# One more tile of attention's result turned by DMA, and three small moves, in a one-core transformer block

## The chip, the cores and the metric

The kernel runs on one core of a Trainium2 chip. The metric is the device time of one execution in microseconds (us); the number that counts is the median of several runs. The profile is of one further execution.

## What is computed

A pre-LayerNorm block over 2048 positions of width 512, all in float32: attention with 32 heads of 16, in which each position looks at 8 positions with a step of 2 (itself and 7 earlier ones), a projection `wo` and a residual; then an MLP of width 1792 with a squared ReLU, and a second residual.

```python
x = A_x
h = x + attention(layernorm(x), A_wqkv) @ A_wo
r = relu(layernorm(h) @ B_w1 + B_b1)
out = h + (r * r) @ B_w2 + B_b2
```

## The kernel before, in words

**Products.** Every float32 matrix is split into a high part (what the engine's float32r type keeps) and a low part (the rest), and a product is three matmul passes: high by high, low by high, high by low (`mm3`, line 231). So every operand needs a cast on ScalarE (`hi`, line 152) and a subtraction on VectorE or GpSimd (`lo`, line 155). The last group of four tiles computes its first MLP product by a Strassen-like scheme in seven products per pair of blocks (`PAIRS`, `products_a`, `products_b`, line 833); for it sums of blocks of `w1` are loaded as `traw`, summed (`t_sums`) and split (`t_split`) into `th` and `tl`, in two halves of the contraction, k = 0 and k = 2.

**Tiles.** The 2048 positions are 16 tiles of 128. First come all of the products of x with `wqkv` (to DRAM, from which attention reads its windows), then groups of four tiles go through the MLP. The attention of tiles 0 to 3 runs under the qkv products of later tiles, and tiles 0 to 3 also go through `wo` there.

**Order.** It is written out by hand. Time is cut into slots; `at`, `midway` and `after` put a chore into a slot (run before, inside or after the attention steps of that slot, by `end_slot`). VectorE's attention steps come from a generator; `pump` takes the next step while a ledger `now["dve"]` is behind `now["pe"]`. Each chore and product adds its cost in us to one of the two; `transposes` adds 0.44 to `now["pe"]` for four transposes. What an engine is given, it executes in that order.

**Turning tiles.** Attention's result `o` and the normalized `h` must be transposed before they can be stationary operands. `o_T` and `h_T` do it on TensorE into PSUM (four transposes of 128x128, line 204); ScalarE then casts the high part, VectorE subtracts for the low part. The other way is by DMA: `turn_split` copies the float32 tile into two planes of 16-bit halves (ScalarE, line 629), `turn_dma` issues a DMA transpose on the SP queue that writes back into the source (line 633), `turn_join` puts the halves together again (ScalarE, line 638), and then cast and subtraction follow from SBUF. The list `OV` names the tiles 4 to 15 that go by DMA for `o`, `HV` those for `h`. Tiles 0 to 3 of `o` go by `o_T` in slots k = 4, 5, 10, 12 (`OT`) of the last two rounds of `first_phase`; their `wo` products stand in slots k = 7, 9, 13, 15 (`WO`). Tile 3's normalized h is turned on TensorE (`h_T`) in slot 23, just before the MLP begins.

**Buffers.** Rows of 128x512 float32 come from one pool of 15 (`row`). Attention's result tiles (two tiles of 128 each), `ohl`, and blocks of `w1` share the tag "o" with three buffers.

**The deviation.** `norm_stats` computes mean and variance on VectorE; its inner `finish` computes the reciprocal deviation on GpSimd in three small instructions (lines 169 to 172) and is placed in the slot's list, for keys 6 and 10 immediately. ScalarE's `norm_apply` (line 199) waits for it.

Of the kernel before, what the change touches and what calls it, by code (L numbers as in the profile page):

```python
# [8 lines left out]
F32 = mybir.dt.float32  # L9
# [6 lines left out]
S, D, H, DH, W, F = 2048, 512, 32, 16, 8, 1792  # L16
P = 128
# [23 lines left out]
WO = 7, 9, 13, 15  # L41
HT = 20, 20, 21, 23
HK = (12, 18), (14, 19)
W2 = (18,)
LH = 3, 4, 10, 11
OP = 6, 7, 12, 13
# [12 lines left out]
def block_kernel(ctx, tc, x, wqkv, wo, w1, b1, w2, b2, out):  # L59
    nc = tc.nc  # L60
# [3 lines left out]
    att = ctx.enter_context(tc.tile_pool(name="att", bufs=2))  # L64
# [37 lines left out]
    def row(name, shape=(P, D), dt=F32):  # L102
        return work.tile(list(shape), dt, name=name, tag="row", bufs=ROWS)
# [9 lines left out]
    def at(delta, fn, *a):  # L113
        due.setdefault(now["slot"] + delta, []).append((fn, a))

    def after(delta, fn, *a):
        late.setdefault(now["slot"] + delta, []).append((fn, a))
# [4 lines left out]
    def end_slot(pe):  # L122
        now["pe"] += pe
        run(due)
        pump()
        run(amid)
        run(late)
        now["slot"] += 1
# [7 lines left out]
    def dve(t):  # L136
        now["dve"] += t
# [13 lines left out]
    def hi(dst, src):  # L151
        nc.scalar.copy(dst, src)  # L152

    def lo(eng, dst, src, h):
        eng.tensor_tensor(out=dst, in0=src, in1=h, op=ALU.subtract)  # L155
# [3 lines left out]
    def norm_stats(key, src, soon=False):  # L159
        st = small.tile([P, 6], F32, name="st")  # L160
        mv = small.tile([P, 2], F32, name="mv", bufs=4)
        rs = small.tile([P, 2], F32, name="rs", bufs=4)
        nc.vector.bn_stats(st, src)
        nc.vector.bn_aggr(mv, st)
        dve(0.93)
        stats[key] = mv, rs

        def finish():
            nc.gpsimd.tensor_scalar(out=rs[:, 1:2], in0=mv[:, 1:2], scalar1=EPS, scalar2=None,
                                    op0=ALU.add)  # L170
            nc.gpsimd.tensor_tensor(out=rs[:, 0:1], in0=rs[:, 1:2], in1=mhalf, op=ALU.pow)
            nc.gpsimd.tensor_scalar(out=rs[:, 1:2], in0=mv[:, 0:1], scalar1=rs[:, 0:1],
                                    scalar2=-1.0, op0=ALU.mult, op1=ALU.mult)
        if key in (6, 10) and soon:
            finish()
        else:
            (at if soon else after)(0, finish)
# [19 lines left out]
    def norm_apply(key, dst, src, eng):  # L197
        mv, rs = stats.pop(key)
        nc.scalar.activation(dst, src, AF.Identity, scale=rs[:, 0:1], bias=rs[:, 1:2])

    def transposes(src, banks="tr"):
        tr = turn[banks].tile("tr").rearrange("p (k c) -> p k c", k=KB)
        for k in range(KB):
            nc.tensor.transpose(tr[:, k, :], src[:, k * P:(k + 1) * P], ident)  # L204
        now["pe"] += 0.44
        return tr
# [213 lines left out]
    def pump(until=None):  # L420

        while (done[until] < G) if until is not None else (now["dve"] < now["pe"]):
            if until is None and now["dve"] > now["pe"] - HALF:
                run(amid)
            todo = sums[:]
            sums.clear()
            t = next(stream, "end")
            for a in todo:
                add_up(*a)
            if t == "end":  # L430
                now["dve"] = 1e9
                return
            if t is None:
                now["dve"] = max(now["dve"], now["pe"])
                return
            dve(t * SLOW[min(now['sub'] + 1, 2)])
# [10 lines left out]
    def x_stats(t):  # L447
        if t < XS:
            norm_stats(t, xt[t])
        else:  # L450
            act_stats(t, xt[t])
# [25 lines left out]
    def x_T(t):  # L477
        tr = transposes(xt.pop(t))
        xT[t] = row("xh", (P, KB, P), F32R), row("xl", (P, KB, P), F32R)
        at(0, hi_T, tr, [xT[t][0]])  # L480
        (midway if t >= 6 else after)(0, lo_T, tr, [xT[t][0]], [xT[t][1]])
# [112 lines left out]
    hs, hn = {}, {}  # L594
# [10 lines left out]
    def o_T(t):  # L605
        s, j = divmod(t, RI)
        pump(until=s)
        tr = transposes(o_t[s][:, j, :])
        if t % R == RI:

            ohl = att.tile([P, 2, KB, P], F32R, name="ohl", tag="o", bufs=3)
            oT[t] = ohl[:, 0], ohl[:, 1]
        else:
            oT[t] = row("oh", (P, KB, P), F32R), row("ol", (P, KB, P), F32R)
        at(0, hi_T, tr, [oT[t][0]])
        at(0, lo_T, tr, [oT[t][0]], [oT[t][1]])

    planes = {}

    def halves_of(a):  # L620
        return a.bitcast(U16).rearrange("p (n two) -> p two n", two=2)

    def two_planes(a):
        return a.bitcast(U16).rearrange("p (two n) -> p two n", two=2)

    def turn_split(key, src):

        planes[key] = src, row("pl")
        nc.scalar.copy(two_planes(planes[key][1]), halves_of(src))

    def turn_dma(key):
        src, pl = planes[key]
        nc.sync.dma_start_transpose(
            src.bitcast(U16).rearrange("p (n c) -> p n c", c=P), pl.bitcast(U16))
# [7 lines left out]
    def o_split(t):  # L642
        s, j = divmod(t, RI)
        pump(until=s)
        turn_split(("o", t), o_t[s][:, j, :])
# [12 lines left out]
    def h_split(t):  # L658
        turn_split(("h", t), hn.pop(t))
# [19 lines left out]
            norm_stats(t, h, R <= t < 14)  # L679

    def h_norm(t):
        hn[t] = row("hn")
        norm_apply(t, hn[t], hs[t], nc.scalar)
        if t >= 14 or t in (6, 10):
            h_split(t)
            turn_dma(("h", t))
# [12 lines left out]
    def wo_product(t, slots):  # L699
        ps = turn["mm"].tile("wo")  # L700
        oh, ol = oT.pop(t)
        mm3(ps, lambda k: oh[:, k, :], lambda k: ol[:, k, :],
            lambda k: wo_h[:, k, :], lambda k: wo_l[:, k, :], lows_last=t in OV)
        for n, (fn, a) in zip(slots, ((h_add, (t, ps)), (h_norm, (t,)), (add_b2, (t,)),
                                      (spill, (t,)))):
            (at if fn is h_add or fn is h_norm and t >= 14
             else midway if fn is h_norm and t in (6, 10) else after)(n + (fn is add_b2), fn, *a)
# [79 lines left out]
    def t_tile(n, name, dt=F32):  # L787
        return att.tile([P, KB, 2, P], dt, name=name, tag=("pr", "o")[n % 2], bufs=3)
# [17 lines left out]
    def t_split(n):  # L806
        h, l = t_tile(n, "th", F32R), t_tile(n, "tl", F32R)
        hi(h, tw[n])
        for k, eng in ((2, nc.gpsimd), (0, nc.vector if n < 3 else nc.gpsimd)):
            lo(eng, l[:, k:k + 2], tw[n][:, k:k + 2], h[:, k:k + 2])  # L810
        tw[n] = h, l

# [193 lines left out]
    for n in range(16):  # L1006
        gp, t = divmod(n, 4)
# [28 lines left out]
    def first_phase(t0):  # L1036
        def chores(m):
            if t0 + 3 < 16:
                if m in (0, 2):
                    at(0, x_stats, t0 + 2 + m // 2)  # L1040

                early = t0 == 12
                if m + early in ((4, 6) if t0 == R else (6, 7)):
                    at(0, x_norm, t0 + 2 + (m + early) // 7 if t0 > R else t0 + m // 2)
                if m in XT[early]:
                    x_T(t0 + 2 + XT[early].index(m))
            if t0 + 5 < 16 and m in (6, 9):
                at(0, load_x, t0 + 2 + m // 3)
            if jobs and m % 3 == 0:
                at(0, weight_job)  # L1050
            k = t0 // 2 * 12 - 72 + m
            if k == 19:
                dve(HOLD)
            for t in range(R):
                if k == OT[t]:
                    at(0, load_h, t)
                    o_T(t)
                if t in HV and k == HK[t][0]:
                    at(0, h_split, t)
                    after(0, turn_dma, ("h", t))  # L1060
                if t in HV and k == HK[t][1]:
                    at(0, turn_join, ("h", t))
                if k == WO[t]:
                    wo_product(t, (1, 3, 4, 6))
                    now["pe"] += 2.73
                if k == HT[t]:
                    (at(0, h_parts, t) if t in HV else h_T(t))
            if k in W2:
                at(0, load_w2, W2.index(k))

        def half(m):
            end_slot(1.37)
            chores(m)

        for n in range(6):
            chores(2 * n)
            qkv_of(t0 + n % 2, n // 2, lambda: half(2 * n + 1))
            end_slot(1.37)
# [40 lines left out]
    for u in range(R - 1):  # L1119
# [11 lines left out]
        for i in js:  # L1131
            t = R * (u + 1) + i
            if not end:
# [23 lines left out]
                p, h = (HP[i], i % 2) if u < 2 else HL[i]  # L1157
# [98 lines left out]
    h = hs[S // P - 1]  # L1256
# [34 lines left out]
```

## Time and profile before

| what | value |
|---|---|
| median of 3 runs | 501.62 us (501.02 to 502.49) |
| the profiled execution, its own time | 501.04 us |
| its span, first to last instruction | 499.2 us |
| TensorE, matmul / weight load | 494.5 us (99%) / 421.4 us (84%) |
| VectorE / ScalarE / GpSimd | 383.5 (77%) / 306.5 (61%) / 355.2 us (71%) |
| granted TensorE clock | 1.000 |

Around the span lie 1.84 us in which no instruction of the program runs. The engine shares are averages over the whole span; the views used further down show single stretches. In a timeline a row is a start, a duration, an engine, a line, an operation, what it writes and reads, and in brackets how long the engine stood idle before it and what ended that.

### The profile page before, as it was taken

To read this page: it belongs to the slowest core of one execution; us is meant where nothing else is said; L and a number is where in the kernel's file an instruction comes from. 1 tells how busy PE (TensorE), PEld (TensorE's weight loads), DVE (VectorE), ACT (ScalarE), POOL (GpSimd) and SP (SyncE) were. 2 spreads that over 40 slices of the span, in tenths; PEclk is the share of its full clock that TensorE was granted. 3 is DMA by queue.
4 is the path that set the end of the run, shared out by engine and by line. 5 is a ranking of instruction groups with operands and counts; after the bars stand their busy time and mean duration, and the time that the engine had idled before them with its cause. 6 is when DMAs were issued, how large, how long until landed. Compare 5 with 4: busy or idle time off the path is not lost.

```text
span 499.2 us, 7516 instructions
## 1 busy us (share of the span) xinstructions
PE 494.5 (99%) x2411; PEld 421.4 (84%) x2411; DVE 383.5 (77%) x526; ACT 306.5 (61%) x543; POOL 355.2 (71%) x429
## 2 busy tenths in 40 slices
PE   8999999999999999999999999999999999999997
PEld 8998888888888888888888888888888888998986
DVE  6379899999989899998979989897984257733233
ACT  5635777768346757478564556866454958766541
POOL 5714898896775999888878777787889353885610
PEclk9999999999999999999999999999999999999999
DMA  8668979879697889589676945977670574355212
GB/s 277 198 225 239 304 233 313 271 253 301 205 235 247 301 280 251 190 233 267 193 253 214 222 137 171 269 232 254 210 197 11 131 200 154 118 157 168 64 42 87
DMA packets 113584, 103.67 MB, mean 208 GB/s; under 512 B 33672, under 2 KB 82056, under 8 KB 113544
## 3 DMA queue, kind: packets, MB, share of 16 engines
q1 hardware_dynamic: 112600, 102.66, 68.4%
q10 hardware_dynamic: 944, 0.52, 0.3%
q8 instruction: 19, 0.31, 0.2%
q14 instruction: 21, 0.17, 0.1%
HBM read 72.65 MB, written 24.25 MB: 194 GB/s over the span
## 4 chain that ended last, share of the span: by engine, by line
PE 98%; POOL 0%; ACT 0%; issue 0%; DVE 0%; POOLq 0%; ACTq 0%
PE mm L231 49%; PE acc L920 30%; PE wo L231 9%; PE mm L833 6%; PE tr L204 2%; PE tr L974 1%; POOL tl L155 0%; PE half L943 0%; ACT th L152 0%; DVE h L945 0%; POOL ident masks.py:199 0%; POOL ident masks.py:197 0%; POOLq masks.py:199 0%; ACTq L152 0%; POOLq L957 0%
## 5 line engine op out<-in xcount | busy, mean ns | idle before, releaser
L414 POOL TENSOR_TENSOR pr<-pr 128x512 f32<-128x512 f32 (+1 forms) x128 | 134.2, 1048 | 35.9 <-DVE pr L357 30.6
L231 PE MATMUL mm<-big_l,w_h 128*128 128x512 f32 x336 | 88.5, 389 | 0.0
L357 DVE TENSOR_TENSOR pr<-ex,v 128x1024 f32<-128x1024 f32 x62 | 75.6, 1221 | 10.7 <-POOL o L414 8.1
L344 DVE TENSOR_TENSOR pr<-qp,k 128x1024 f32<-128x1024 f32 x64 | 76.8, 1201 | 5.7 <-ACT qp L271 3.5
L380 DVE TENSOR_REDUCE ex<-pr 128x64 f32<-128x1024 f32 x64 | 78.4, 1225 | 1.8
L231 PEld LDWEIGHTS mm<-big_l,w_h 128*128 128x128 f32 x336 | 63.0, 188 | 13.4 <-ACT r L890 0.3
L155 POOL TENSOR_TENSOR rl<-r,rh 128x512 fp32r<-128x512 f32 x42 | 54.9, 1308 | 24.0 <-ACT rh L152 20.0
L231 PE MATMUL mm<-big_l,xh 128*128 128x512 f32 (+1 forms) x208 | 56.2, 378 | 0.0
L231 PE MATMUL mm<-big_h,xh 128*128 128x512 f32 (+1 forms) x208 | 53.1, 377 | 0.0
L231 PE MATMUL mm<-big_h,xl 128*128 128x512 f32 (+1 forms) x208 | 52.5, 374 | 0.0
L920 PE MATMUL acc<-big_l,rh 128*128 128x512 f32 x190 | 52.0, 390 | 0.0
L920 PE MATMUL acc<-big_h,rh 128*128 128x512 f32 x190 | 51.9, 390 | 0.0
L920 PE MATMUL acc<-big_h,rl 128*128 128x512 f32 x190 | 51.7, 389 | 0.0
L231 PE MATMUL mm<-big_l,w_l 128*128 128x512 f32 x168 | 44.9, 389 | 0.0
L231 PEld LDWEIGHTS mm<-big_h,xl 128*128 128x128 f32 x208 | 38.3, 188 | 5.9
L231 PEld LDWEIGHTS mm<-big_h,xh 128*128 128x128 f32 x208 | 38.0, 188 | 5.6 <-ACT xh L152 0.2
L920 PEld LDWEIGHTS acc<-big_h,rl 128*128 128x128 f32 x190 | 35.7, 188 | 7.4
L920 PEld LDWEIGHTS acc<-big_l,rh 128*128 128x128 f32 x190 | 35.6, 188 | 7.4
L231 PEld LDWEIGHTS mm<-big_l,xh 128*128 128x128 f32 x208 | 37.5, 188 | 4.9
L920 PEld LDWEIGHTS acc<-big_h,rh 128*128 128x128 f32 x190 | 35.1, 188 | 6.8
L890 ACT ACTIVATE r<-mm,b_sb 128x512 f32<-128x512 f32 x42 | 28.8, 685 | 16.1 <-PE mm L231 15.2
L536 ACT COPY y<-mm 128x512 f32<-128x512 f32 x36 | 21.1, 587 | 26.5 <-PE mm L231 23.2
(162 smaller groups left out, 931.7 us busy)
## 6 DMA issues: line engine op xcount, KB each, us to landing
k<-qkv_d SPq DMA_DIRECT2D x50, 288.0 KB, 3.8
v<-qkv_d SPq DMA_DIRECT2D x46, 288.0 KB, 2.8
qkv_d<-y SPq DMA_DIRECT2D x18, 512.0 KB, 3.8
big_l<-w2l_d SPq DMA_DIRECT2D x24, 256.0 KB, 2.8
xt<-in_A_x_dram SPq DMA_DIRECT2D x16, 256.0 KB, 4.1
q<-qkv_d SPq DMA_DIRECT2D x32, 128.0 KB, 3.6
h<-in_A_x_dram SPq DMA_DIRECT2D x16, 256.0 KB, 3.3
h_d<-h SPq DMA_DIRECT2D x16, 256.0 KB, 3.4
```

Source lines behind the costliest of these rows:

```text
L155: eng.tensor_tensor(out=dst, in0=src, in1=h, op=ALU.subtract)
L204: nc.tensor.transpose(tr[:, k, :], src[:, k * P:(k + 1) * P], ident)
L231: nc.tensor.matmul(ps, l(k), r(k), start=(n == 0), stop=(n == 3 * KB - 1))
L344: nc.vector.tensor_tensor(out=pr.rearrange("p i w h d -> p i w (h d)"), in0=qps["now"][:, j % 2].unsqueeze(2).to_broadcast([P, RI, W, GC]) ...
L357: nc.vector.tensor_tensor(out=p2, in1=vwin, op=ALU.mult, in0=e1[:, :, :, j * GH:(j + 1) * GH].unsqueeze(4).to_broadcast([P, RI, W, GH, DH]))
L380: nc.vector.tensor_reduce(out=lf[:, :, :, j * GH:(j + 1) * GH], in_=pr, axis=X, op=ALU.add)
L414: nc.gpsimd.tensor_tensor(out=dst, in0=p2[:, :, :w], in1=p2[:, :, w:2 * w], op=ALU.add)
L536: nc.scalar.copy(dst, src)
L833: nc.tensor.matmul(ps, sta[y][:, k], mov[x][:, k], start=(first and q == 0), stop=(last and q == len(terms) - 1), skip_group_check=True)
L890: nc.scalar.activation(r, ps, AF.Relu, bias=b1_sb[:, f:f + 1])
L920: nc.tensor.matmul(acc[j], l[:, j * P:(j + 1) * P], w[f], start=(first and n < len(js)), stop=(last and n >= len(terms) - len(js)))
L974: nc.tensor.transpose(warm[:, n % KB, :], ident, ident)
```

## The change

Tile 3's `o` no longer goes by `o_T` in slot 12: its planes are split after slot 9 and sent to the DMA transpose, and joined after slot 12; its low part moves from slot 12 to slot 13. Tile 6's normalized h and its planes lie in one buffer of the tag "o" instead of two rows. The deviation of tiles 7 and 11 is issued at once, ahead of what else is listed in its slot. In `t_split` the half k = 2 goes to VectorE (for the first three pairs) and the half k = 0 to GpSimd, where it was the other way.

```diff
+OK = {3: (9, 12)}
@@ norm_stats
-        if key in (6, 10) and soon:
+        if key in (6, 7, 10, 11) and soon:
             finish()
         else:
             (at if soon else after)(0, finish)
@@
-    planes = {}
+    planes, spare = {}, {}
@@ turn_split
-        planes[key] = src, row("pl")
+        planes[key] = src, spare.pop(key) if key in spare else row("pl")
         nc.scalar.copy(two_planes(planes[key][1]), halves_of(src))
@@ h_norm
-        hn[t] = row("hn")
+        if t == 6:
+            two = att.tile([P, 2, D], F32, name="hnp", tag="o", bufs=3)
+            hn[t], spare["h", t] = two[:, 0], two[:, 1]
+        else:
+            hn[t] = row("hn")
@@ t_split
-        for k, eng in ((2, nc.gpsimd), (0, nc.vector if n < 3 else nc.gpsimd)):
+        for k, eng in ((2, nc.vector if n < 3 else nc.gpsimd), (0, nc.gpsimd)):
             lo(eng, l[:, k:k + 2], tw[n][:, k:k + 2], h[:, k:k + 2])
@@ first_phase, chores
             for t in range(R):
                 if k == OT[t]:
                     at(0, load_h, t)
-                    o_T(t)
+                    if t not in OK:
+                        o_T(t)
+                if t in OK and k == OK[t][0]:
+                    after(0, o_split, t)
+                    after(0, turn_dma, ("o", t))
+                if t in OK and k == OK[t][1]:
+                    after(0, o_join, t, 1)
```

## Rows read from the trace of the kernel before

**Rows 1.** The page: busy time of the engines, and the chain by engine.
```profile
PE 494.5 (99%) x2411; PEld 421.4 (84%) x2411; DVE 383.5 (77%) x526; ACT 306.5 (61%) x543; POOL 355.2 (71%) x429
...
PE 98%; POOL 0%; ACT 0%; issue 0%; DVE 0%; POOLq 0%; ACTq 0%
```

**Rows 2.** Waits by pair: who waited for whom, us in total, times, longest.
```profile
PE mm L833 <- POOL tl L155: 0.2, 1, 0.2
```

**Rows 3.** The chain in order of time (start, us, what), at tile 3's turn.
```profile
136.50 0.44 PE tr L204 x4
```

**Rows 4.** Timeline of TensorE in the last group of tiles.
```profile
427.32 0.40 PE L833 MATMUL mm<-big_l,w_h 128*128 128x256 f32 x2
427.56 0.40 PE L833 MATMUL mm<-big_l,th 128*128 128x256 f32 x2
428.13 0.51 PE L833 MATMUL mm<-big_l,tl 128*128 128x256 f32 x2 [0.17 <-POOL tl L155]
428.47 0.40 PE L833 MATMUL mm<-big_l,th 128*128 128x256 f32 x2
```

**Rows 5.** The chain in order of time, just before that.
```profile
425.15 1.06 ACT th L152
...
426.28 1.81 POOL tl L155
```

**Rows 6.** Timeline of VectorE, the same stretch.
```profile
426.23 0.69 DVE L155 TENSOR_TENSOR tl<-traw,th 128x512 fp32r<-128x512 f32 x1 [0.80 <-ACT th L152]
...
427.97 2.47 DVE L928 TENSOR_TENSOR h<-acc,h 128x512 f32<-128x512 f32 x4
```

**Rows 7.** Instructions by tile (o, oh, ol): ns min/median/max; landing in us.
```profile
L638 ACT COPY pl<-o x12: 1164/1168/1175, 195.7 to 393.7; 128x1024 uint16<-128x1024 uint16 x12
...
DMA to landing us min/median/max: 4.5/4.5/5.3
...
L152 ACT CAST oh<-pl x9: 620/622/624, 197.0 to 394.9; 128x512 fp32r<-128x512 f32 x9
...
L155 DVE TENSOR_TENSOR ol<-pl,oh x9: 681/960/1819, 199.0 to 395.6; 128x512 fp32r<-128x512 f32 x9
L155 DVE TENSOR_TENSOR ol<-tr,oh x3: 680/691/692, 119.1 to 138.6; 128x512 fp32r<-128x512 f32 x3
```

**Rows 8.** Timeline of ScalarE around slots 9 to 21.
```profile
133.33 0.59 ACT L536 COPY y<-mm 128x512 f32<-128x512 f32 x1 [4.10 <-PE mm L231]
...
137.02 1.05 ACT L629 COPY pl<-hn 128x1024 uint16<-128x1024 uint16 x1
...
152.16 0.82 ACT L199 ACTIVATE hn<-h,rs 128x512 f32<-128x512 f32 x1
```

**Rows 9.** Timeline of GpSimd: tile 3's o complete, and tile 3's deviation.
```profile
115.80 0.47 POOL L414 TENSOR_TENSOR o<-pr 128x128 f32<-128x128 f32 x1
...
151.30 0.27 POOL L172 TENSOR_SCALAR rs<-mv,rs 128x1 f32<-128x1 f32 x1
```

**Rows 10.** Timeline of the SP queue: the load that follows slot 9.
```profile
132.67 0.38 SPq L603 DMA_DIRECT2D h<-in_A_x_dram  x1
```

**Rows 11.** Timeline of VectorE from tile 3's low part to the MLP's first product.
```profile
138.59 0.69 DVE L155 TENSOR_TENSOR ol<-tr,oh 128x512 fp32r<-128x512 f32 x1 [1.85 <-ACT oh L152]
139.20 1.22 DVE L357 TENSOR_TENSOR pr<-ex,v 128x1024 f32<-128x1024 f32 x1
...
153.03 1.23 DVE L380 TENSOR_REDUCE ex<-pr 128x64 f32<-128x1024 f32 x1
154.88 2.95 DVE L155 TENSOR_TENSOR big_l<-pl,big_l 128x256 fp32r<-128x256 f32 x4 [0.62 <-ACT big_l L152]
...
159.54 0.74 DVE L155 TENSOR_TENSOR big_l<-tr,big_l 128x256 fp32r<-128x256 f32 x2
```

**Rows 12.** Timeline of TensorE: tile 3's wo product, the MLP's first third pass.
```profile
143.61 1.07 PE L231 MATMUL wo<-wo_h,oh 128*128 128x512 f32 x4
...
161.35 1.98 PE L231 MATMUL mm<-big_l,w_h 128*128 128x512 f32 x8
```

## The prediction

> **What bounds the kernel now.** First the engines' busy times and the chain that ended last [rows 1]: TensorE is busy 494.5 of 499.2 us, and 98% of the chain is TensorE. So only two things can shorten this kernel: work taken off TensorE, or a place where TensorE stands. The table of waits is read next, for such places: outside the start-up it has one, the product that reads `tl`, with 0.2 us [rows 2]. Then the stretches around the edits: the chain at tile 3's turn [rows 3], the last group's first blocks on TensorE, in the chain and on VectorE [rows 4 to 6], and each engine between slot 9 and the MLP's first product [rows 8 to 12]. There the question is by how much each operand of TensorE comes before it is needed, since a wait that is not there yet is in no table. The granted clock is 1.000 and TensorE never rests for long, so the clock is no term.
>
> **Change 1, tile 3's turn.** Removed: four transposes, 0.44 us of the chain [rows 3], and all of it on the path, since TensorE runs without a gap there. Added: a split (1.05 us for the same copy of a tile, [rows 8]), a DMA transpose that lands 4.5 to 5.3 us after its issue, a join of 1.17 and a cast of 0.62 [rows 7]; gone from ScalarE is the cast out of PSUM. I follow the new chain through the queues:
> - Split: `o` of tile 3 was complete at 116.27, so the forced `pump` in `o_split` does nothing. ScalarE is idle for 4.10 us before 133.33 [rows 8, 9], so the split costs nobody anything, if its row is free by then.
> - The DMA goes ahead of the load of tile 2's h at 132.67 on the SP queue [rows 10] and lands at about 132.7 + 4.5 = 137.2, or 138.0 at the slowest. The load behind it moves by the time of one issue; it is used four slots on.
> - Join: ScalarE does tile 0's split (137.02), tile 1's `hn` (0.82 like the one at 152.16, directly behind it since the cast in between is gone), then the join from about 138.7 and the cast, until 138.7 + 1.17 + 0.62 = 140.5. ScalarE waits for TensorE after that, so this is hidden.
> - The low part is one VectorE instruction as before. Out of PSUM it took 0.69; out of SBUF, where both inputs now lie, 0.68 to 1.82, median 0.96 [rows 7]. I take the median: it ends at 141.5, against 139.28. `wo` of tile 3 begins at 143.61 on TensorE [rows 12], now at 143.17, so both parts are still on time.
>
> What is late next is VectorE's own queue. In its order the attention step at 139.20 now goes ahead of the low part, and then VectorE stands until 140.5. Both were done at 140.42 [rows 11] and are done at 141.5 now: a lag of 1.1 us for all that follows.
>
> Then the planner. The ledger `now["pe"]` is 0.44 lower from slot 12 on, so an attention step that was taken with less than 0.44 to spare goes to the next slot. I added up the code's own costs slot by slot: this happens in about fifteen of the 55 slots that are left of attention, mostly with nothing of VectorE's in between. One place matters. In slot 19 a reduce was taken with 0.03 to spare (the row at 153.03). Now it comes only in slot 21, behind the low parts of tiles 0 and 1 (the row at 154.88) and of tile 2, so that the low part of tile 3 (the row at 159.54) starts about 1.17 us later, the time from the start of a reduce to the start of what follows [rows 11]. That is an operand of the MLP's first product. Its third pass begins at 161.35 [rows 12], which becomes 160.91.
>
> The lag of 1.1 is mostly used up before: the reduce that moves away (1.23) and the idle 0.62 make room for it on VectorE. But tile 3's deviation depends on VectorE as well: GpSimd ended it at 151.57 [rows 9], ScalarE took `hn` at 152.16 behind a join [rows 8]. It would now end near 152.3 (1.1 later, less a reciprocal step of about 0.3 that the ledger moves behind it), some 0.15 late. So tile 3's low part starts at 159.54 + 1.17 + 0.15 = 160.86; its first half ends at 161.27 against a need at 160.91. **TensorE stands for about 0.4 us** there. Bounds: 0 (the lag vanishes and the order doesn't matter) and 1.3 (the low part takes the largest 1.82 and the lag goes through in full).
>
> One rule of the Trainium skill bears on that low part: "SBUF — State Buffer", section Who interferes with whom, says that a VectorE instruction with two SBUF inputs contends with a GpSimd instruction that reads SBUF and is locked out for the whole of it. The spread from 0.68 to 1.82 in [rows 7] agrees with it; taken at its worst the low part takes 0.86 us more than I assume, and the sum at the end would be a loss of 0.42 instead of a gain of 0.44; that belongs to the slower rival.
>
> **Change 2, the halves of `tl`.** In the second block of the last group the product that comes second reads the half k = 2. The two instructions that make the halves start together behind the cast `th`: GpSimd takes 1.81 [rows 5], VectorE 0.69 [rows 6]. TensorE's pairs of matmuls follow each other every 0.24 us (427.32 to 427.56); so the row after next should begin at 428.04 and begins at 428.47 [rows 4]: the stand costs 0.43 us, more than the 0.17 that the gap says. With VectorE on the half k = 2 it is there at 426.92, before it is needed at 427.80. GpSimd's half, at 428.09, is first read three pairs or 0.72 us later than the other, at 428.52. So the 0.43 goes. What is next: VectorE's additions of the finished accumulators end at 430.44 [rows 6], and the products that follow write those four banks again, some 0.24 us apart; I allow 0.03 for the last of them and take **0.40 us**, with bounds 0 and 0.43. Elsewhere the exchange changes only who makes a half that is ready in time.
>
> **Changes 3 and 4.** The early deviation of tiles 7 and 11: TensorE waits for no `hn` in the table of waits, so an earlier one gains nothing [rows 2]. The low part of r that now stands behind it comes later by three small instructions, the last of which takes 0.27 [rows 9]; it is read by a product three slots on, which covers that. Tile 6's buffer: same copies, same lengths; the tag "o" has a free one at that time, and two rows become free. Both at nothing. If their cover were gone, the first would cost its three instructions (some 1.1 us, an estimate from that last one), the second one copy of 1.05 [rows 8].
>
> **The sum.** -0.44 - 0.40 + 0.40 = -0.44 us. The profiled execution took 501.04, 0.58 below the median of 501.62; I subtract from the median: **501.2 us**.
>
> **The rivals.**
> - *No stand at the MLP's start.* The lag is absorbed, both gains are kept: 501.62 - 0.84 = 500.8. For it: VectorE has idle time on both sides of the moved steps [rows 11]. Against it: the low part of tile 3 would have to start 0.4 us earlier than my count.
> - *Nothing arrives.* TensorE is early but is held again later, by VectorE's attention steps before the `wo` products, where they run nearly back to back, and by the additions in [rows 6]. Then both gains are given back: 501.6. For it: VectorE is the busiest engine after TensorE, at 77% [rows 1]. Against it: each `h_add` waits for the end of its own `wo` product, so VectorE is tied to TensorE there and moves along.
> - *Slower.* The DMA way is the longer one, about 8.3 us from the split to the low part (1.05 + 4.5 + 1.17 + 0.62 + 0.96) against 1.7 (0.44, 0.59 as the copy out of PSUM at 133.33, 0.69), and it begins too late. The planes need one of the 15 rows, which are all in use in slot 9; the next ones come free as TensorE goes through tile 1's `wo` product and the qkv product whose copy begins at 133.33 [rows 8]. With the last of these the split ends at 134.5, the planes land at 139.1 to 139.9 and the low part ends, at 0.96 to 1.82 for itself, 0.4 to 2.0 us after 141.5. Each us goes through VectorE, the deviation and `hn` of tile 3 to the MLP's first product. It decides from 141.9 on, 0.44 late, where both gains are used up; at 1.4 us late it is 501.2 + 1.4 = 502.6. By the Trainium skill, "VectorE: DVE Perf Modes", section Rules for kernel authors, a 128x128 transpose belongs on TensorE where a result in PSUM is acceptable, and to the DMA otherwise; here PSUM was acceptable, and the landing of 4.5 us against 0.44 in [rows 3, 7] is on the rule's side. It is the cover of three slots that speaks against it.
>
> **How the numbers follow.** Forecast (a stand of some 0.4 us, 500.9 to 501.5): 0.45. No stand, 500.8: 0.25. Nothing arrives, 501.6: 0.13. Slower, 502.6: 0.17. A measurement of this kernel can tell about 0.3% from no change, which is 1.5 us here; none of the first three reaches that, and the slower one reaches it only if that low part is nearly 2 us late. What makes a median 1.5 us faster would be the 0.84 and a run that is favourable by 0.7, as the three shown are spread. So faster 0.08, same 0.84, slower 0.08. Range: 500.3 (both gains in full and 0.5 of spread) to 502.7 (the slower case).
>
> **What would show it.** After: TensorE has four transposes fewer, the MLP's first product begins 0.44 earlier, and its third pass is preceded by an idle time that ends with VectorE's `big_l<-tr`, some 0.4 long. The low part of tile 3's `o` reads `pl` and ends at 141 to 142. The wait for `tl` is gone from TensorE's table. The prediction is wrong if the DMA lands after 138.7, if VectorE keeps its old order after slot 19, or if a new wait of TensorE stands anywhere after 165 us.

## The result and the profile after

| kernel | median (runs) | runs | ratio to before, 95% interval |
|---|---|---|---|
| before | 501.66 us (501.02 to 503.36) | 9 | |
| changed | 502.97 us (502.68 to 504.55) | 9 | 1.0037 (1.0028 to 1.0046) |

The change makes the kernel 1.3 us slower; 501.2 was forecast, with 502.7 as the upper end. The profiled execution of the changed kernel took 503.04 us with a span of 501.3, against 501.04 and 499.2 before.

The table of TensorE's waits comes first (engine, tile and line that waited, what released it: us in total, times, longest). Line numbers of the changed kernel are a few higher than before.

```profile
PE tr L979 <- POOL ident masks.py:199: 1.3, 1, 1.3
PE mm L232 <- ACT r L895: 0.5, 1, 0.5
PE tr L205 <- ACT hn L200: 0.4, 1, 0.4
PE mm L232 <- DVE big_l L156: 0.3, 1, 0.3
PE mm L232 <- ACT xh L153: 0.2, 1, 0.2
```

The wait for `tl` [rows 2] is gone. Three new ones stand in its place, for `r`, `hn` and `big_l`, and only the one for `big_l` was forecast; the row for `xh` is of the start-up, at 7.3 us. Comparing the starts of the same matmuls in both traces gives the whole account of TensorE; its differences are larger than the waits in the table, since the starts behind a stand are further apart as well (161.30 and 161.63 for 161.35 and 161.58):

| at (us, before) | what TensorE meets there | after minus before |
|---|---|---|
| 137 | four transposes fewer | -0.44 |
| 161.4 | VectorE's low part of tile 3's h, for the MLP's first product | +0.50 |
| 167.7 | a PSUM bank, freed by ScalarE's evacuation into `r` | +0.79 |
| 245.2 | ScalarE's `hn` of tile 7, for its transposes | +0.66 |
| 248.9, 336 | tile 7's low part; tile 11's low part | +0.27, +0.12 |
| 428.1 | `tl` is ready | -0.40 |
| 430.9 | a finished accumulator's bank | +0.18 |
| sum | the last matmul | +1.68 |

At 336 us the profile names no releaser. The second half of VectorE's row ends at 338.49, just before the second matmul of that pass, at 338.56; in the kernel before the low part was done at 335.09, for a need at 336.66 (the kernel before, then the changed one):

```profile
334.35 0.74 DVE L155 TENSOR_TENSOR big_l<-tr,big_l 128x256 fp32r<-128x256 f32 x2
...
337.75 0.74 DVE L156 TENSOR_TENSOR big_l<-tr,big_l 128x256 fp32r<-128x256 f32 x2
```

The first 12 us of a run vary by up to 0.2 either way, which is left out of such differences below. The rest of the difference of the spans, 0.4, lies behind the last matmul, in the last transfer; it varies between 3.4 and 3.8 us among the kernels here.

**At 161 and 167 us.** VectorE's timeline after (start, duration, line, operation, output and inputs, count, and the idle time before it with what ended it), to be held against [rows 11] (GpSimd, named for the 2.73, is the wrong releaser, as shown further down):

```profile
140.60 0.75 DVE L156 TENSOR_TENSOR ol<-pl,oh 128x512 fp32r<-128x512 f32 x1 [2.73 <-POOL pr L415]
141.27 1.22 DVE L381 TENSOR_REDUCE ex<-pr 128x64 f32<-128x1024 f32 x1
...
158.58 1.21 DVE L381 TENSOR_REDUCE ex<-pr 128x64 f32<-128x1024 f32 x1
159.71 1.21 DVE L345 TENSOR_TENSOR pr<-qp,k 128x1024 f32<-128x1024 f32 x1
160.84 0.74 DVE L156 TENSOR_TENSOR big_l<-tr,big_l 128x256 fp32r<-128x256 f32 x2
161.50 1.21 DVE L358 TENSOR_TENSOR pr<-ex,v 128x1024 f32<-128x1024 f32 x1
```

The reduce that stood at 153.03 stands at 158.58, ahead of tile 3's low part, which starts at 160.84 instead of 159.54. That is the stand at 161. The same lateness goes on to the weighing `pr<-ex,v`, at 161.50 instead of 160.21, and from there by a way that the prediction did not follow. The chain of waits that ends with the stand at 167 (start, length, what):

```profile
161.57 1.14 DVE pr L358
162.72 0.02 issue
162.73 0.32 SPq L251
163.05 0.05 issue
163.10 4.04 DMA raw<-in_B_w_dram
167.15 0.02 issue
167.17 0.62 ACT big_h L153
167.79 0.59 ACT r L895
168.39 0.04 issue
168.43 0.73 PE mm L232 x2
```

The weighing frees the buffer of `v`; SP's queue stands on the next load of `v` until then; the load of `w2`'s second row is queued behind it; ScalarE stands for that row; and the evacuation that frees TensorE's bank is queued on ScalarE behind the cast. No link of this is an operand of TensorE; the last one gives it a bank. In the kernel before, the same load and ScalarE's two steps were:

```profile
161.82 0.42 SPq L1082 DMA_DIRECT2D raw<-in_B_w_dram  x1
165.52 0.62 ACT L152 CAST big_h<-raw 128x512 fp32r<-128x512 f32 x1 [1.05 <-DMA raw<-in_B_w_dram]
166.04 0.69 ACT L890 ACTIVATE r<-mm,b_sb 128x512 f32<-128x512 f32 x1
```

So the cast is 1.65 later (167.17 for 165.52): the load was issued 1.28 later, and the time from its issue to the cast was 0.37 longer. Only the first part follows from the weighing; a run below bears on the second.

**At 245 us.** VectorE, GpSimd and ScalarE after:

```profile
231.35 0.69 DVE L675 TENSOR_TENSOR h<-wo,h 128x512 f32<-128x512 f32 x1 [1.18 <-PE wo L232]
...
232.91 1.19 DVE L358 TENSOR_TENSOR pr<-ex,v 128x1024 f32<-128x1024 f32 x1
...
239.82 1.23 DVE L345 TENSOR_TENSOR pr<-qp,k 128x1024 f32<-128x1024 f32 x1 [1.75 <-POOL o L415]
...
241.56 0.68 DVE L675 TENSOR_TENSOR h<-wo,h 128x512 f32<-128x512 f32 x1
...
242.74 1.30 POOL L156 TENSOR_TENSOR rl<-r,rh 128x512 fp32r<-128x512 f32 x1
244.12 0.23 POOL L170 TENSOR_SCALAR rs<-mv 128x1 f32<-128x1 f32 x1
...
245.84 0.81 ACT L200 ACTIVATE hn<-h,rs 128x512 f32<-128x512 f32 x1 [1.55 <-POOL rs L173]
```

In the kernel before, a weighing filled the time in which VectorE waited for tile 6's `wo` product, and `hn` came at 243.50:

```profile
228.95 1.21 DVE L357 TENSOR_TENSOR pr<-ex,v 128x1024 f32<-128x1024 f32 x1
230.49 0.69 DVE L674 TENSOR_TENSOR h<-wo,h 128x512 f32<-128x512 f32 x1 [0.34 <-PE wo L231]
...
238.65 0.69 DVE L674 TENSOR_TENSOR h<-wo,h 128x512 f32<-128x512 f32 x1 [0.40 <-PE wo L231]
...
243.50 0.82 ACT L199 ACTIVATE hn<-h,rs 128x512 f32<-128x512 f32 x1 [1.26 <-POOL rs L172]
```

Now VectorE is idle there for 1.18 us, the weighing comes behind tile 6's `h_add`, GpSimd's additions of its products come later too, a dot step waits 1.75 us for them, and tile 7's `h_add`, queued behind it, comes 2.9 us later (241.56 for 238.65). `hn` of tile 7 follows at 245.84 instead of 243.50.

### The profile page after: what moved, and what is told of

It reads as the page before. It is cut to its first block, busy times and chain, and to the rows that moved or that the text cites. A ratio compares the mean times of both kernels' runs of the same rounds, so it can differ in the third digit from the quotient of the medians.

```text
span 501.3 us, 7510 instructions
## 1 busy us (share of the span) xinstructions
PE 495.0 (99%) x2407; PEld 420.5 (84%) x2407; DVE 381.6 (76%) x526; ACT 307.5 (61%) x545; POOL 354.3 (71%) x429
## 4 chain that ended last, share of the span: by engine, by line
PE 63%; POOL 2%; DVE 1%; DMA 1%; ACT 0%; issue 0%; SPq 0%; POOLq 0%
PE acc L925 28%; PE mm L232 21%; PE mm L838 7%; PE wo L232 6%; POOL pr L415 1%; DMA raw<-in_B_w_dram 1%; POOL rl L156 1%; DVE pr L358 0%; PE half L948 0%; POOL rs L172 0%; DVE pr L345 0%; PE tr L205 0%; POOL rs L173 0%; POOL o L415 0%; ACT hn L200 0%
## 5 line engine op out<-in xcount | busy, mean ns | idle before, releaser
L232 PEld LDWEIGHTS mm<-big_l,w_l 128*128 128x128 f32 x168 | 31.5, 188 | 6.6
```

The costliest lines, as they stand in the source:

```text
L232: nc.tensor.matmul(ps, l(k), r(k), start=(n == 0), stop=(n == 3 * KB - 1))
```

## The experiments

The theory A: the turn by DMA is hidden, but the 0.44 that it takes out of the planner's ledger `now["pe"]` puts VectorE's attention steps into another order, and that order makes the stands. The rival B: the turn itself does it, by its lag, its place in the queues or its traffic. The runs were made on three chips, each with runs of the kernel before beside it, so ratios are compared. A trace shows one execution; a stand in it may be missing from another.

**The ledger put back, the turn kept.** VectorE's order is then that of before, instruction for instruction in the two traces.

```diff
                     if t not in OK:
                         o_T(t)
+                    else:
+                        now["pe"] += 0.44
```

> The changed kernel, with the 0.44 us of tile 3's four transposes still counted in the planner's ledger in slot 12, though TensorE no longer does them: VectorE's attention steps stand in the order of before, and the turn by DMA and the other changes stay. Theory A (the ledger, and with it VectorE's order, makes the loss): the stands at 161, 167 and 246 us are gone or under 0.15 us each, both gains stay, and the time is 501.66 - 0.44 - 0.40 + 0.2 (the new stand at 430 us) = 501.0, 500.7 to 501.4. Rival B (the turn by DMA is too slow or its traffic and its place in the queues hold others up): the stands at 161 and 167 stay as in the changed kernel, 0.5 and 0.8 us, and the time is 502.4 to 503.0.

501.31 us, ratio 1.0005 (0.9996 to 1.0014). The stands at 161, 167 and 245 us are gone, so B falls as their cause. But TensorE gains only some 0.3 us in all, where 0.66 was to be expected (0.44 + 0.40 - 0.18): the 0.44 of the transposes was given back in small pieces, 0.24 of it at 159.4 us. The row that begins there in this run follows VectorE's low part of tile 2 by 0.15 us. VectorE is late, and its timeline shows since when:

```profile
136.75 1.22 DVE L358 TENSOR_TENSOR pr<-ex,v 128x1024 f32<-128x1024 f32 x1
140.69 0.76 DVE L156 TENSOR_TENSOR ol<-pl,oh 128x512 fp32r<-128x512 f32 x1 [2.73 <-POOL pr L415]
141.37 1.22 DVE L381 TENSOR_REDUCE ex<-pr 128x64 f32<-128x1024 f32 x1
```

The 2.73 is put down to GpSimd, but the low part needs ScalarE's cast `oh`, which ended at 140.60 here:

```profile
139.98 0.62 ACT L153 CAST oh<-pl 128x512 fp32r<-128x512 f32 x1
```

**The ledger alone.** The kernel before, with the turn on TensorE:

```diff
                     o_T(t)
+                    if t == 3:
+                        now["pe"] -= 0.44
```

> The kernel before, with nothing changed but the ledger: 0.44 us are taken off it in slot 12 after tile 3's turn, which stays on TensorE. All of the computation and all other orders are those of before. Theory A: VectorE's order is that of the changed kernel; the stand at 161 us is small (no lag of the low part, and TensorE comes 0.44 us later: 0 to 0.1), the stands at 167 and at 246 us come, 0.3 to 0.8 and 0.7 to 1.5 us: 502.3 to 503.3. Rival B: the order of VectorE's steps costs nothing by itself: 501.5 to 501.8.

502.68 us, ratio 1.0021 (1.0009 to 1.0034). A number in the ledger, with nothing taken from or given to any engine, costs 1.3 us by the medians beside it (501.38). VectorE's order in this trace is that of the changed kernel, tile 3's own low part apart. There is no stand at 161, one of 0.55 at 167, and one of 0.9 at 236 us, before tile 7's `wo` product:

```profile
PE wo L231 <- ACT oh L152: 0.7, 1, 0.7
...
PE mm L231 <- ACT r L890: 0.2, 1, 0.2
```

The loss is the one expected; its second place is another one, 10 us earlier than in the changed kernel. There the cast waits for tile 7's turn by DMA:

```profile
229.27 6.04 DMA o<-pl
...
235.32 1.18 ACT L638 COPY pl<-o 128x1024 uint16<-128x1024 uint16 x1 [2.10 <-DMA o<-pl]
```

That turn is issued at 226.39 in the kernel before, at 229.27 here and at 229.47 in the changed kernel, where it landed after 4.4 us instead of 6.0 and TensorE did not stand for it. So the order delays two things in this stretch, the turn and tile 7's `h_add`; in this trace TensorE met the first, in the changed kernel's the second.

**The other edits without the turn.** `OK = {}`.

> The changed kernel with tile 3's result turned on TensorE as before; the exchange of tl's halves, tile 6's planes in an attention buffer and the early deviation stay. Theory A: order of before, so no stand at 161, 167 or 246 us; only the exchange acts, -0.40 and +0.2: 501.4, 501.2 to 501.6. Rival B: the same. Rival C (tile 6's buffer makes the stand at 246 us): that stand is there, 0.7 us or more: 502.0 to 502.8.

501.10 us, ratio 0.9999 (0.9987 to 1.0011), which can't be told from no change. In the trace TensorE runs level with the kernel before up to 428 us, then gains 0.41 and gives back 0.19. So tile 6's buffer makes no stand. The early deviation of tiles 7 and 11 has no run of its own; this trace has GpSimd's instructions in the order of before throughout, so the change moved nothing there.

**One reduce put back.** With `dve(HOLD - 0.44)` in slot 19 and 0.44 taken off again at the MLP's start, VectorE's order differs from the changed kernel's in one place:

```diff
+L381 ex<-pr
 L156 big_l<-pl,big_l x4
 L156 big_l<-tr,big_l x2
-L381 ex<-pr
```

> The changed kernel, in which one step alone is put back: the reduce that the lower ledger moved from slot 19 to slot 21 stands again ahead of the low parts of tiles 0, 1 and 2 on VectorE. From the MLP's start on the ledger is as low as in the changed kernel, and VectorE's order there is the same. Theory A (two places in the order, each with its own stand): tile 3's low part is on time and the weighing behind it is early again, so the stands at 161 and 167 us go, 1.2 to 1.3 us together; that at 246 us stays with 0.6 to 0.9: 501.7, 501.4 to 502.1. Rival D (it is not that one step but the lag of the low part from the DMA turn that makes the first two stands): they stay, 0.4 us or more at 161 and 0.5 or more at 167: 502.5 to 503.0.

502.34 us, ratio 1.0023 (1.0014 to 1.0033). Half of the expectation failed: the stand at 161 is gone, the one at 167 stays with 0.74. The weighing is back at 160.71 and the load of `w2`'s row is issued at 162.32, 0.8 earlier than in the changed kernel; yet ScalarE still waits for it until 166.76:

```profile
166.76 0.62 ACT L153 CAST big_h<-raw 128x512 fp32r<-128x512 f32 x1 [2.60 <-DMA raw<-in_B_w_dram]
167.29 0.68 ACT L895 ACTIVATE r<-mm,b_sb 128x512 f32<-128x512 f32 x1
```

So the reduce explains 161 and not 167. Up to there VectorE, ScalarE and SP's queue have the same order as in the run with the ledger put back, which has no stand; only three additions of GpSimd, all before 151 us, come in another place. The load was issued 0.2 earlier than there (162.32 for 162.53), and its reader began 4.44 us after the issue instead of 3.58. In this run it is the load's time that makes the stand, and the weighing isn't needed for it. What stands behind the load is tested by itself next.

Between 230 and 250 us, where 0.6 to 0.9 was expected at one place, this trace loses 0.77 at three: 0.26 at a pass of tile 7's `wo` product at 238, 0.17 at `hn`, and 0.34 at tile 7's low part.

**The cast behind that load, one slot later,** in the changed kernel:

```diff
-                    after(0, split_w2, p)
+                    after(1 if p == 1 else 0, split_w2, p)
```

> The changed kernel, in which only the splitting of w2's second row (ScalarE's cast and the two steps behind it) comes one slot later, so that ScalarE evacuates the next PSUM bank before it waits for that row's load. Theory A (at 167 us TensorE stands because that evacuation is queued on ScalarE behind a cast that waits for a late load): the stand at 167 us (0.8 us) is under 0.15, that at 161 us (0.5) and that at 246 us stay; 502.97 - 0.6 to 0.8 = 502.2 to 502.4, if nothing is made up for at 246 us. Rival G (the evacuation itself or its product is late): the stand at 167 us stays at 0.5 or more: 502.7 to 503.1.

502.12 us, ratio 1.0011 (1.0002 to 1.0019), a little under the time expected. The stand at 167 is gone and the other two are there, so the link from the load over ScalarE's queue to TensorE's bank holds. The evacuation now stands ahead of the cast:

```profile
165.44 0.69 ACT L895 ACTIVATE r<-mm,b_sb 128x512 f32<-128x512 f32 x1 [0.73 <-PE mm L232]
...
167.67 0.62 ACT L153 CAST big_h<-raw 128x512 fp32r<-128x512 f32 x1
```

**The ledger put back at the MLP's start only** (`now["pe"] += 0.44` ahead of its loop):

> The changed kernel, with the 0.44 us put back into the planner's ledger only where the MLP begins: up to there VectorE's order is that of the changed kernel, from there on that of before. Theory A (two separate places in the order): the stands at 161 and 167 us stay, so that TensorE is some 0.85 us later than in the kernel before at 168 us; the one at 246 us goes; with the exchange (-0.40 + 0.18) that makes +0.63 on the time before: 502.1, 501.9 to 502.4. Rival E (the stand at 246 us is the late echo of those at 161 and 167): it stays, 0.5 us or more: 502.7 to 503.0.

502.21 us, ratio 1.0003 (0.9994 to 1.0012). The stands at 161 (0.54 by the starts of the matmuls) and 167 (0.86) stay, that at 245 is gone: it comes from the order of the steps after the MLP's start, not as an echo of the first two. The time agrees with the expectation; the ratio of the chip's runs is so near to 1 because the kernel before had a median of 501.87 beside it. Its trace is of the slowest of its eleven executions (502.80) and has 0.7 of its own at 323 us, where a `wo` product waits for a turn by DMA.

**The halves of tl undone** in the changed kernel (`t_split` as before):

> The changed kernel with the halves of tl made by the engines of before; all else as changed. Theory A (the exchange takes 0.40 us at 428 us and gives back 0.18 at 431): the wait for tl is back, no stand for VectorE's h at 430.9 us beyond that of before: 502.97 + 0.2 = 503.2, 503.0 to 503.4. Rival H (the 0.40 arrives in full): 503.4; rival I (all of it is given back): 503.0.

503.33 us over six runs, ratio 1.0031 (1.002 to 1.0043), by the medians 0.36 more than the changed kernel's and by the ratios no more (1.0031 for 1.0037): the times can't separate the three cases. The traces do, though this one is of the slowest of the six, with 1.3 at 167: the wait for `tl` is back, and the 0.18 at 431 us is gone.

**The low part one slot later on VectorE,** with the ledger put back:

```diff
-                    after(0, o_join, t, 1)
+                    after(0, o_join, t, 2)
```

> The changed kernel with the ledger kept as it was before (as in the run with the ledger put back) and one instruction moved on VectorE: the low part of tile 3's o comes one slot later, behind five attention steps instead of ahead of them. In the run with the ledger put back VectorE stood 2.72 us for ScalarE's cast there, and was 0.7 us late at the MLP's start. Theory A, next part (the turn by DMA costs nothing by itself; its low part in the wrong place of VectorE's queue made the lag that ate the 0.44): the stand of 2.7 us at 138 us is gone or under 0.5, the low part ends by 142.6, before TensorE's need at about 143.2, and TensorE is still 0.35 to 0.44 us earlier than in the kernel before at 168 us; time before minus 0.6: 500.8, 500.5 to 501.1. Rival F (the lag comes from elsewhere, or others wait just as long): TensorE is no more than 0.2 us earlier at 168 us, as in that run: 501.1 to 501.4.

500.82 us, ratio 0.9980 (0.9971 to 0.9989): faster than both kernels, by 1.0 us on this ratio, of which TensorE's starts show 0.66. VectorE no longer stands:

```profile
136.85 1.21 DVE L358 TENSOR_TENSOR pr<-ex,v 128x1024 f32<-128x1024 f32 x1
138.10 1.23 DVE L381 TENSOR_REDUCE ex<-pr 128x64 f32<-128x1024 f32 x1
139.36 0.43 DVE L390 TENSOR_TENSOR ex<-ex,mask 128x256 f32<-128x256 f32 x1
139.83 1.22 DVE L358 TENSOR_TENSOR pr<-ex,v 128x1024 f32<-128x1024 f32 x1
140.97 0.41 DVE L398 TENSOR_REDUCE mx<-ex 128x32 f32<-128x256 f32 x1
141.42 0.43 DVE L400 TENSOR_TENSOR ex<-ex,mx 128x256 f32<-128x256 f32 x1
141.76 1.59 DVE L156 TENSOR_TENSOR ol<-pl,oh 128x512 fp32r<-128x512 f32 x1
```

Five steps that had been ready ran in the time of the wait, and TensorE keeps the 0.44 up to 428 us and gains 0.66 in all. The low part took 1.59 instead of 0.76 and ended at 143.35, later than the 142.6 of the expectation, but TensorE reads it only at 144.24, in the product's second pass:

```profile
144.24 1.07 PE L232 MATMUL wo<-wo_h,ol 128*128 128x512 f32 x4
```

**The low part later, with the lowered ledger.**

> The changed kernel with its lowered ledger, and only the low part of tile 3's o one slot later on VectorE, behind the attention steps. With the changed kernel, the run with the ledger put back and the run with both, it fills the square of two causes: the ledger's order and the place of the low part. Theory A (the ledger's order is the larger loss: alone it cost 1.3 us): the stand at 161 us is under 0.2, that at 167 us 0.5 or more is there, some 0.5 or more between 230 and 250 us as well: 502.2 to 502.8. Rival J (the lag from the misplaced low part was the larger, and the order hurts only a VectorE that is late): 500.8 to 501.5.

502.66 us, ratio 1.0027 (1.0018 to 1.0036). The trace has 0.6 at 167 and 0.6 at 245, as theory A has it. It is of the slowest of twelve executions (504.14) and has 0.5 more at 323 and 1.2 more at 336. The square of the two causes, as ratios to before:

| | ledger lowered | ledger as before |
|---|---|---|
| low part ahead of five steps | 1.0037 (the change) | 1.0005 |
| low part behind them | 1.0027 | 0.9980 |

With the lowered ledger two of the five steps also change places with an `h_add`. The ledger is worth 0.32 and 0.47% in the two rows, the place of the low part 0.10 and 0.25% in the two columns. The larger one is the ledger, and rival J falls. The 0.10 is not told from nothing, as the two intervals overlap; of the 0.25 (1.3 us) TensorE's starts show 0.35, and the rest is not placed. With the low part later there is no stand at 161, nor with the ledger alone or the reduce put back: that one needs the lag and the moved reduce together.

**One addition ahead of tl's half,** in the faster version:

```diff
-            at(u // 2, finish, R * u + i, acc[i])
+            at(u // 2 if i else 0, finish, R * u + i, acc[i])
```

> The version with the ledger as before and the low part later, in which one of the four additions of the finished accumulators stands on VectorE ahead of tl's half, in the 0.8 us for which VectorE waits for ScalarE there. Theory A (the exchange of tl's halves gives back 0.18 us at 431 us because the last addition comes too late for the product that writes its bank again): TensorE has no stand at 430 us, its last matmul comes 0.1 to 0.2 earlier than in that version, 500.82 - 0.15 = 500.7, 500.4 to 500.9. Rival (the bank is not what the product waits for, or the early addition pushes tl's half back onto the path): unchanged or later, 500.8 to 501.3.

500.43 us, ratio 0.9981 (0.9973 to 0.9990). In the trace the additions end earlier and TensorE gives nothing back at 431 us, so what it had met there was the end of the additions. The time can't be told from the version without it, and the trace does not end earlier either, since it has 0.55 at 323 us, where a `wo` product waits for a turn by DMA.

```profile
425.45 0.68 DVE L933 TENSOR_TENSOR h<-acc,h 128x512 f32<-128x512 f32 x1
426.34 0.69 DVE L156 TENSOR_TENSOR tl<-traw,th 128x512 fp32r<-128x512 f32 x1 [0.21 <-ACT th L153]
...
428.07 1.88 DVE L933 TENSOR_TENSOR h<-acc,h 128x512 f32<-128x512 f32 x3
```

**The cast later as well,** in the faster version without that:

> The version with the ledger as before and the low part later, and the splitting of w2's second row one slot later as well. If ScalarE's wait for that load costs nothing where VectorE is on time: 500.8, 500.6 to 501.0. If the load's landing holds TensorE in part of the runs even there: 500.5 to 500.7.

500.62 us, ratio 0.9986 (0.9977 to 0.9995): no different, and both cases of the expectation allow 500.62. Where VectorE is on time, ScalarE's wait for that load costs nothing that these runs can tell.

## Why the prediction was wrong

**What was right.** The four transposes gave 0.44 where they stood. The new chain ran within 0.2 us of the steps written down: the planes' DMA was issued at 132.67, the join ran at 138.69, the cast ended at 140.51 and the low part at 141.35 (forecast 132.7, 138.7, 140.5, 141.5). The reduce did move from slot 19 to slot 21, tile 3's low part started at 160.84 (forecast 160.86), and the stand there was 0.50 for 0.4. That the start fits to 0.02 is luck in part: the 0.15 in it was to come through tile 3's deviation and `hn`, but `hn` began at 152.18 for 152.16, and the 0.15 came from the low parts of tiles 0 and 1, which took 3.10 for 2.95. The exchange of `tl` took 0.40 at its place.

**The step that failed** is "Then the planner", in its sentence "One place matters". Fifteen moved steps were counted, and one was priced: the one with an operand of TensorE behind it on VectorE. The others were put at nothing with "mostly with nothing of VectorE's in between", and not one was followed to who reads its result or waits for its buffer. The reason does not hold in the traces: fourteen attention steps of the changed kernel come behind at least one more of VectorE's other instructions than before, eight of them behind three or more. The two stands left out cost 1.45 us: 0.79 at 167, over SP's queue, a load and ScalarE's queue, and 0.66 at 245, over tile 7's `h_add`. With the 0.39 that follow they are 1.84, more than the whole 1.68 lost. The run with the ledger alone loses 1.58 on TensorE, without tile 3's turn. That the lowered ledger makes this loss is shown by the two runs on it. That the first stand begins with the weighing that frees `v` is read from the trace of the changed kernel, and the run with the one reduce put back has the stand without it; that the second begins with the weighing that no longer fills VectorE's idle time ahead of tile 6's `h_add` is read from the trace too. The prediction named its own sign: "a new wait of TensorE stands anywhere after 165 us".

**The lag** of VectorE, 1.1 by the prediction's count and 0.82 in the changed kernel (141.27 for 140.45), was called "mostly used up before" the MLP. With the reduce gone that was right: the low parts began at 154.89 for 154.88. Where the ledger was put back and the reduce stayed, it was 0.7 at the weighing (160.92 for 160.21), and it took most of change 1's gain. The prediction saw VectorE stand until 140.5 and did not ask what ready work was queued behind: five steps, 3.7 us, as the faster version shows.

**Two terms.** The additions at 431 us were allowed 0.03; they cost 0.18, since the first of them starts behind three steps of the products and all four follow each other in 2.47 us [rows 6]. Change 3 was read as placing the low part of r behind the deviation; it moves nothing, as r's low part was and is ahead of it (242.74 and 244.12 after).

**The rivals.** "Slower" gave 502.6, near the measured 502.97, for a reason that did not occur: its low part had to end after 141.9, and it ended at 141.35. Its remark on the rows was right (the split waited for TensorE's `wo` product until 131.08), and the cover of three slots held. "Nothing arrives" came true for change 1 in the run with the ledger put back. The Trainium skill's rule on two SBUF inputs ("SBUF — State Buffer", section Who interferes with whom) lets the one of the two engines that begins second wait for the other; the prediction gave VectorE the loss whichever began first. The low part took 0.75 in the changed kernel and 1.59 in the faster version, on time in both, and the traces agree with the rule (the last section has the numbers); the 1.82 that the prediction took for its worst case is the largest of [rows 7]. The 5.3 taken as the slowest landing was of too few turns: ScalarE waited in the trace of before for one until 6.86 us after its issue (314.07 to 320.94). Tile 3's had 6.02 (132.67 to 138.69), so this cost nothing.

**What stays open.** Why ScalarE's cast at 167 comes 3.6 to 4.6 us after the issue of its load (below). Every trace with the ledger lowered before the MLP and the cast in its place has the stand there, 0.5 to 1.3 us, and none with the ledger of before has it; how the ledger leads to it is not shown. Open too is which of the moved steps after the MLP's start makes the one at 245: the weighing is read from the traces, and only the order of that whole stretch was tried.

## What to carry to other kernels

Where a planner with a ledger sets the order, an edit that changes a cost changes every decision after it: list the two orders side by side, and either price every moved step by who reads its result and who waits for its buffer, or keep the ledger's number as it was. Where an operand comes later, put its reader behind the work that is ready on that in-order engine; five steps of VectorE that stood behind one low part decided here whether the 0.44 us arrived. Slack of DMA loads and of the copies that free banks belongs in the count like slack of TensorE's operands.

## What the runs showed of the hardware

The load of one row of `w2` (256 KB), issued directly behind the same load of `v`, let ScalarE's waiting cast begin 3.70 us after its issue in the kernel before (161.82 to 165.52), 4.07 in the changed one, 4.44 with the one reduce put back, 4.62 with the halves of `tl` undone and 3.58 with the ledger put back, though the order of transfers around it is the same. The five traces with the ledger of before in which the cast waits for the load have 3.58 to 4.07, the six with a lowered one 4.00 to 4.62; what makes the difference is not shown.

The turn by DMA ahead of the `wo` product at 323 us held SP's queue for 3.11 to 3.54 us in ten traces and for 4.04 to 4.29 in the three (the ledger put back at the MLP's start, the low part later with the lowered ledger, one addition early) in which TensorE stood there, for 0.48 to 0.74 us.

The low part of tile 3, the same VectorE instruction on the same kinds of tiles, took 0.75, 0.76 and 1.59 us in the changed kernel, with the ledger put back and in the faster version. Each time an addition of GpSimd was running when it began, and the low part ended 0.54 to 0.55 us after that addition (which ended at 140.80, 140.91 and 142.81). Where none was running, the same kind of low part took 0.68, and an addition that began 0.16 later took 1.67 us instead of 1.29 (287.09 and 287.25 in the kernel before). So the one that began second waited, on either engine.
